# One unit's normed x turned by DMA instead of TensorE, its matmuls one slot later, hash signs behind an eviction

## The chip, the core and the metric

The kernel runs on one core of one Trainium2 chip. Its metric is device time in microseconds: the median of the runs of one program. All numbers without a unit are microseconds. PE is TensorE (PEld its weight loads), DVE is VectorE, ACT is ScalarE, POOL is GpSimd, SP is SyncE, which here issues DMAs.

## The reference

An attention whose scores are masked by a hash, followed by a feed-forward layer. Cut to what is computed:

```
q_bits = (q @ proj > 0); k_bits = (k @ proj > 0)      # 6 bits per token and head
mask   = bucket(q_bits)[:, None] == bucket(k_bits)[None, :]
attn   = softmax(where(mask, q @ k.T / sqrt(64), -1e9))
x      = (attn @ v) of all 8 heads side by side        # 3072 x 512
xn     = x / sqrt(mean(x * x) + 1e-6) * rms_g
out    = (silu(xn @ w_gate) * (xn @ w_val)) @ w_out    # 512 -> 1536 -> 512
```

q, k and v are 4 batches x 8 heads x 768 tokens x 64; everything is f32 outside, f16 in the matmuls inside.

## The kernel before, in words

The work is cut into eight *units* of 384 tokens (half of a batch's 768), numbered 0 to 7. For each unit there is an attention stage of 8 heads and a feed-forward stage.

*Attention.* q and k are loaded by SP, turned so that the 64 features lie on partitions (on TensorE for the first pairs of heads, by DVE for the others: `turn_dve`), and cast to f16 by POOL into the tiles QK. Under the 64 features stand six rows with the hash's sign bits, so that one matmul gives scores and mask together. `hash_one` makes these rows for a pair of heads: four small f32 matmuls into a PSUM bank `d_ps`, one DVE instruction (`signs`) that keeps the sign of each number as f16 (`bits`), and eight small DMAs on SP that put the six rows in place. `scores` is two matmuls into a PSUM tile `s_ps` (two of these tiles exist), `probs` one softmax exponential on ACT (`psb`), `av` eighteen small matmuls for each head into `o_ps` (one such tile), `attn_out` an addition and a reciprocal on DVE (`otmp`, `rcp`) and a product on POOL (`x`).

*Feed-forward.* `norm` takes the sums of squares, a power on POOL and three DVE multiplies that write `xn` (f16, tokens on partitions, one third of 128 tokens at a time). `turn_x` turns one third with four TensorE transposes into a PSUM bank `x_ps`, and moves it into `xnT` while multiplying by rms_g, which lies along partitions in `gcol`. `gate` and `value` are 4 matmuls each for one of 12 column blocks (`g_ps`, `v_ps`, halves of two matmuls), a tanh on ACT (`t`) and two DVE instructions (`a`, `ht`). `project` is 12 matmuls for each third (`y_ps`), `store` a copy on ACT (`ysb`, three buffers) and a DMA on SP. d_ps, x_ps, g_ps, v_ps, y_ps and the mean's m_ps share three PSUM banks in turn.

*What sets the order.* The program is written out in order; each engine runs its own instructions in that order and waits on semaphores. The main loop runs over 192 *slots*, one for each third of a head (two of the six key blocks). A slot emits the scores of the next slot, the exponential of this one, and then what the table `plan` holds for it. While the attention of unit u+1 runs (24 slots from `t0 = NS * (u + 1)`), unit u - 1 is projected and unit u's gates and values are made: first nine pieces of four matmuls of `project(u - 1)`, three for each third, with the turns of unit u behind the seventh and eighth, then 48 half gates and half values of unit u. `spread` deals these pieces to the slots so that each slot gets about the same planned TensorE time; the means and the hashes (`inserts`) are put between pieces at their due slots. The list `late` holds steps that stand behind everything else of their slot, `attn_out` (`o_step`) among them. `norm(u)` stands in slot t0 + 4. Behind the loop come the last products, and unit 7's norm, turn and feed-forward.

SP's queue is in order too: loads, hash rows and stores, each issued when its turn has come and its semaphores allow.

Of the kernel before, what the change touches and what calls it, by code (L numbers as in the profile page):

```python
# [8 lines left out]
FP32 = mybir.dt.float32  # L9
FP16 = mybir.dt.float16  # L10
U16 = mybir.dt.uint16
AF = mybir.ActivationFunctionType
ALU = mybir.AluOpType
# [6 lines left out]
DMODEL = H * D  # L20
DFF = 1536
NF = DFF // 128
HALF = 384
# [10 lines left out]
def kernel(  # L34
# [12 lines left out]
    nc = tc.nc  # L47
    PSUM = bass.MemoryType.PSUM

    const = ctx.enter_context(tc.tile_pool(name="const", bufs=1))  # L50
# [4 lines left out]
    npool = ctx.enter_context(tc.tile_pool(name="npool", bufs=1))  # L55
# [16 lines left out]
    mhalf = const.tile([128, 3], FP32, name="mhalf")  # L72
    ssp = [const.tile([128, 5, 3], FP32, name=f"ssp{i}") for i in range(2)]
    gcol = const.tile([128, 4], FP32, name="gcol")
    wg = const.tile([128, 4, DFF], FP16, name="wg")
    wv = const.tile([128, 4, DFF], FP16, name="wv")
    wo = const.tile([128, NF, DMODEL], FP16, name="wo")
# [5 lines left out]
    def bank(name, shape=None, dt=FP32):  # L83
        return gps.tile(shape or [128, 512], dt, name=name, tag="g")
# [126 lines left out]
    def hash_half(parts):  # L211

        ps = bank("d_ps", [128, HALF])
        for t, src in parts:
            nc.tensor.matmul(  # L215
                ps[32 * t : 32 * t + 32, :], pj[:, 0:32], src,
                start=True, stop=True, tile_position=(0, 32 * t),
            )
        return ps

    def signs(dst, ps):

        upper = ps.bitcast(U16).rearrange("p (c two) -> p c two", two=2)[:, :, 1]
        nc.vector.tensor_scalar(
            out=dst.bitcast(U16), in0=upper, scalar1=SIGN, scalar2=BIT,
            op0=ALU.bitwise_and, op1=ALU.bitwise_or,
        )
# [15 lines left out]
    def hash_direct(b, hp, heads):  # L243
# [34 lines left out]

        return sign, direct, move, send

    def hash_one(b, hp):

        where = ((0, "k", 0), (1, "q", 0), (2, "k", 1), (3, "q", 1))
        ps = hash_half(
            [(t, (qT if which == "q" else kT)[b, hp][:, half * HALF : (half + 1) * HALF])
             for t, which, half in where]
        )
        bt = spool.tile([128, HALF], FP16, name="bits")
        signs(bt, ps)
        for hh in range(2):  # L290
            for t, which, half in where:
                o = (0 if which == "q" else S) + half * HALF
                p0 = 32 * t + 6 * hh
                nc.sync.dma_start(
                    out=QK[b, 2 * hp + hh, "h"][D:KROWS, o : o + HALF],
                    in_=bt[p0 : p0 + 6, :],
                )
# [28 lines left out]
    x, xn, xnT = {}, {}, {}  # L326
# [82 lines left out]

    rstds = {}  # L410

    def norm_scale(u):

        ss = spool.tile([128, 3], FP32, name="ss")
        nc.vector.tensor_reduce(
            out=ss, in_=ssp[u % 2].rearrange("p h c -> p c h"), op=ALU.add, axis=AX.X
        )
        rstd = spool.tile([128, 3], FP32, name="rstd")
        nc.gpsimd.tensor_tensor(out=rstd, in0=ss, in1=mhalf, op=ALU.pow)  # L419
        rstds[u] = rstd  # L420

    def norm(u):
        if u not in rstds:
            norm_scale(u)
        xn[u] = npool.tile([128, 3, DMODEL], FP16, name="xn")
        for c in range(3 if u else 2):
            norm_third(u, c, nc.vector.tensor_scalar_mul)

    def norm_third(u, c, mul):
        mul(xn[u][:, c, :], x[u][:, c, :], rstds[u][:, c : c + 1])  # L430
# [131 lines left out]
    NS = 24  # L562
# [5 lines left out]
    def at(w, s, f, *a):  # L568
        plan[NS * w + s].append(lambda: f(*a))
# [70 lines left out]
    at(0, 1, load_natural, nc.sync, 0, 3, "q")  # L640
    at(0, 2, load_v, nc.sync, 0, 2)
    at(0, 2, load_v, nc.sync, 0, 3)
    at(0, 6, v_prep, 0, 1)
    at(0, 15, v_prep, 0, 2)
    at(0, 19, v_prep, 0, 3, nc.vector)
# [37 lines left out]
    for i, t in ((0, 39), (1, 41), (2, 57), (3, 61)):  # L683
        at(0, t, zero_rows, i)
    TX = 37
    sqs = {}

    def o_step(u, hp, *eng):
# [9 lines left out]
    late = []  # L698
    for n, (u, h) in enumerate(order):
        t = 3 * n + 4 - ((u, h) == (0, H - 1))  # L700
        for part in range(2):
            at(0, t + part, av, u, h, part)
        if h % 2:
            if (u, h) == (0, H - 1):

                at(0, t + 1, o_step, u, h // 2, nc.vector)
                at(0, t + 1, norm_scale, u)
                at(0, t + 1, nc.vector.tensor_scalar_mul, gcol, gcol, float(DMODEL) ** 0.5)
                at(0, t + 2, hash_only, 1, 1)
                at(0, t + 2, hash_signs, 1, 1)  # L710
                at(0, t + 2, norm, u)
                at(0, TX-1, norm_third, u, 2, nc.scalar.mul)
                at(0, TX + 1, send_pair, 1, 1)
                for c in range(3):
                    at(0, TX, turn_x, u, c, c == 2)
                continue
            if (u, h) == order[-1]:
                at(0, t + 1, o_step, u, h // 2, nc.vector)
                continue

            steps = [(t + 1, o_step), (t + (6 if h < 7 else 3), s_step)]
            for s, step in steps:
                if s < 2 * NS or s % NS in (2, 4):
                    at(0, s, step, u, h // 2)
                else:
                    late.append((s, step, u, h // 2))
# [14 lines left out]

    SCORES, AV, PROJ, FEED, TURN, HASH, MEAN = 330, 290, 216, 324, 220, 1000, 120
    inserts = {spot[3]: (HASH, hash_one, *pair) for pair, spot in spots.items()}
    for b in (1, 2, 3):
        for s, hp in ((5, 0), (18, 2)):
            assert 2 * b * NS + s not in inserts
            inserts[2 * b * NS + s] = (MEAN, v_mean, b, hp, 4)

    def spread(t0, n, pieces):
        fixed = [SCORES + (AV if (t - 1) % 3 < 2 else 0) for t in range(t0, t0 + n)]  # L750
        extra = [(t, *inserts.pop(t)) for t in range(t0, t0 + n) if t in inserts]
        total = sum(fixed) + sum(p[0] for p in pieces) + sum(e[1] for e in extra)
        i, done = 0, 0
        for s in range(n):
            done += fixed[s]
            while i < len(pieces):
                weight, whole, steps = pieces[i]
                full = done + weight // 2 > total * (s + 1) // n
                if extra and whole and t0 + s >= extra[0][0] and (full or extra[0][1] > MEAN):
                    _, weight, *step = extra.pop(0)  # L760
                    at(0, t0 + s, *step)
                    done += weight
                    continue
                if full:
                    break
                done += weight
                for delay, *step in steps:
                    at(0, t0 + s + delay, *step)
                i += 1
        for _, _, *step in extra:  # L770
            at(0, t0 + n - 1, *step)
        assert i == len(pieces)

    for u in range(7):
        gates = [
            (FEED, f is gate and part == 0, [(0, f, u, ft, part)])
            for ft in range(NF) for f in (gate, value) for part in range(2)
        ]
        if u == 0:
            t0 = TX + 1  # L780
            spread(t0, 2 * NS - t0, gates)
            continue
        t0 = NS * (u + 1)
        at(0, t0 + 4, norm, u)
        pieces = []
        for i in range(9):
            c, n = divmod(i, 3)
            steps = [(0, project, u - 1, c, 4 * n, 4 * n + 4)]
            if n == 2:
                steps.append((1, store, u - 1, c))  # L790
            pieces.append((4 * PROJ, True, steps))
            if i in (6, 7):
                pieces += [
                    (TURN, False, [(0, turn_x, u, c)]) for c in ((0,), (1, 2))[i - 6]
                ]
        spread(t0, NS, pieces + gates)
    for t, (_, *step) in inserts.items():
        at(0, t, *step)

    for t, *step in late:  # L800
        at(0, t, *step)
# [1 line left out]
    def behind_norm(t):  # L803

        return t - t % NS + 7 if 1 <= t % NS < 7 else t

    for (b, hp), (load, kturns, qturns, _) in spots.items():
# [3 lines left out]
        for w, turns in (("k", kturns), ("q", qturns)):  # L811
            for i, t in enumerate(turns):
                at(0, t, turn_dve, b, hp, w, i, len(turns))
            t = turns[-1] + 1
            at(0, t if (b, hp) == (1, 2) else behind_norm(t), cast_pool, b, hp, w)
        t = 54 if (b, hp) == (1, 2) else behind_norm(qturns[-1] + 2)
# [19 lines left out]
    for c in range(2):  # L836
        project(6, c, 0, NF)
        store(6, c)
    norm(7)
    project(6, 2, 0, 4)  # L840
    for c, f0, f1 in ((0, 4, 6), (1, 6, 8), (2, 8, NF)):
# [41 lines left out]
```

## Time and profile before

| | us |
|---|---|
| median of 3 runs (331.27 to 331.42) | 331.28 |
| the profiled execution, its own time | 330.52 |
| its span, first to last instruction | 328.7 |
| PE busy | 323.0 |
| DVE, ACT, POOL busy | 239.5, 227.2, 158.4 |
| four transposes of x (x_ps) in a row, issue to end | 0.39 |
| move of a turned third on DVE (xnT), median | 0.69 |

A row of the timeline gives start, length, engine, line, operation and tiles; "xN" is how many like instructions were merged in it. The number in square brackets is the idle time of that engine ahead of the row, with what ended it. Matmuls overlap in a pipeline: the length of a merged row is from the first one's start to the last one's end, and the distance of the starts is the time that each takes of PE. Times in the trace count from the span's start. The profiled execution's own time is 1.8 over its span and 0.76 under the median of the other runs.

### The profile page before, as it was taken

To read this page: it belongs to the slowest core of one execution; us is meant where nothing else is said; L and a number is where in the kernel's file an instruction comes from. 1 tells how busy PE (TensorE), PEld (TensorE's weight loads), DVE (VectorE), ACT (ScalarE), POOL (GpSimd) and SP (SyncE) were. 2 spreads that over 40 slices of the span, in tenths; PEclk is the share of its full clock that TensorE was granted. 3 is DMA by queue.
4 is the path that set the end of the run, shared out by engine and by line. 5 is a ranking of instruction groups with operands and counts; after the bars stand their busy time and mean duration, and the time that the engine had idled before them with its cause. 6 is when DMAs were issued, how large, how long until landed. Compare 5 with 4: busy or idle time off the path is not lost.

```text
span 328.7 us, 7869 instructions
## 1 busy us (share of the span) xinstructions
PE 323.0 (98%) x2999; PEld 196.6 (60%) x2999; DVE 239.5 (73%) x526; ACT 227.2 (69%) x331; POOL 158.4 (48%) x204
## 2 busy tenths in 40 slices
PE   8999999999999999999999999999999999999995
PEld 3676666656565566656566565655566566665554
DVE  5887877859888778967888568876768455685860
ACT  7999886766678677775768667785767767744321
POOL 4999759955974542824674521755462111221000
PEclk9999999999999999999999999999999999999999
DMA  7943999988139554432816136001000010002002
GB/s 236 335 158 99 225 211 191 184 157 142 70 58 165 118 114 87 73 77 82 164 21 133 36 93 117 7 3 68 34 5 3 34 64 2 0 2 96 3 1 97
DMA packets 79614, 30.93 MB, mean 94 GB/s; under 512 B 64908, under 2 KB 76632, under 8 KB 79576
## 3 DMA queue, kind: packets, MB, share of 16 engines
q1 hardware_dynamic: 75672, 25.65, 33.2%
q0 software_dynamic: 3680, 4.72, 8.5%
q8 instruction: 23, 0.38, 0.5%
q14 instruction: 15, 0.12, 0.1%
q10 hardware_dynamic: 224, 0.07, 0.1%
HBM read 28.32 MB, written 6.29 MB: 105 GB/s over the span
## 4 chain that ended last, share of the span: by engine, by line
PE 97%; ACT 1%; issue 0%; DVE 0%
PE s_ps L335 20%; PE g_ps L454 19%; PE v_ps L454 19%; PE y_ps L483 18%; PE o_ps L360 11%; PE d_ps L215 2%; PE t_ps L155 2%; PE d_ps L235 2%; PE x_ps L437 2%; PE z_ps L550 1%; ACT psb L347 1%; PE y_ps L502 1%; PE m_ps L319 1%; DVE kT L157 0%; PE s_ps L155 0%
## 5 line engine op out<-in xcount | busy, mean ns | idle before, releaser
L347 ACT ACTIVATE psb<-s_ps,ebias 128x768 f16<-128x768 f32 x192 | 167.7, 899 | 20.8 <-PE s_ps L335 19.9
L335 PE MATMUL s_ps<-QK 128*128 128x384 f16 (+1 forms) x384 | 93.5, 326 | 1.2 <-ACT psb L347 1.1
L462 ACT ACTIVATE t<-g_ps 128x384 f32<-128x384 f32 x96 | 47.1, 491 | 53.0 <-PE g_ps L454 52.9
L454 PE MATMUL g_ps<-xnT,wg 128*128 128x384 f16 x384 | 82.6, 326 | 0.0
L454 PE MATMUL v_ps<-xnT,wv 128*128 128x384 f16 x384 | 81.8, 326 | 0.0
L471 DVE SCALAR_TENSOR_TENSOR a<-t,g_ps 128x384 f32<-128x384 f32 x96 | 52.9, 551 | 27.6 <-ACT t L462 26.0
L381 POOL TENSOR_TENSOR x<-otmp,rcp 128x384 f32<-128x384 f32 x30 | 25.1, 835 | 95.5 <-DVE rcp L379 95.3
L483 PE MATMUL y_ps<-wo,ht 128*128 128x512 f16 x276 | 68.0, 379 | 0.0
L472 DVE SCALAR_TENSOR_TENSOR ht<-a,v_ps 128x384 f16<-128x384 f32 x96 | 53.2, 554 | 11.2 <-PE v_ps L454 2.9
L360 PEld LDWEIGHTS <-psb 128*128 128x128 f16 x1152 | 51.9, 97 | 15.7 <-issue 1.2
L360 PE MATMUL o_ps<-vl,psb 128*128 128x65 f16 x1152 | 55.8, 193 | 0.0
L335 PEld LDWEIGHTS <-QK 128*128 128x128 f16 (+1 forms) x384 | 34.6, 98 | 34.3 <-issue 9.2
L454 PEld LDWEIGHTS <-wv 128*128 128x128 f16 x384 | 35.3, 97 | 21.2 <-issue 0.2
L454 PEld LDWEIGHTS <-wg 128*128 128x128 f16 x384 | 34.8, 97 | 20.8 <-DVE xnT L443 0.4
L483 PEld LDWEIGHTS <-ht 128*128 128x128 f16 x276 | 24.8, 98 | 22.4
L495 ACT COPY ysb<-y_ps 128x512 f32<-128x512 f32 x23 | 13.5, 585 | 19.6 <-PE y_ps L483 19.6
L374 DVE TENSOR_TENSOR otmp<-o_ps,cvb 128x390 f32<-128x390 f32 x32 | 17.8, 557 | 7.6 <-PE o_ps L360 7.6
L207 POOL CAST QK<-qT 64x768 f16<-64x768 f32 x20 | 16.4, 820 | 13.4 <-DVE qT L194 12.8
L430 DVE TENSOR_SCALAR xn<-x,rstd 128x512 f16<-128x512 f32 x23 | 15.8, 738 | 6.8 <-POOL rstd L419 6.8
L387 POOL TENSOR_TENSOR sq<-x 128x384 f32<-128x384 f32 x24 | 19.8, 826 | 1.9
L443 DVE TENSOR_TENSOR xnT<-x_ps,gcol 128x512 f16<-128x512 f16 x22 | 14.5, 686 | 8.0 <-PE x_ps L437 7.9
L207 POOL CAST QK<-kT 64x768 f16<-64x768 f32 x20 | 16.4, 820 | 6.6 <-DVE kT L194 4.7
(83 smaller groups left out, 284.5 us busy)
## 6 DMA issues: line engine op xcount, KB each, us to landing
vn<-in_v_dram SPq DMA_DIRECT2D x16, 384.0 KB
out_dram<-ysb SPq DMA_DIRECT2D x23, 256.0 KB
qL<-in_q_dram SPq DMA_DIRECT2D x40, 96.0 KB
kL<-in_k_dram SPq DMA_DIRECT2D x40, 96.0 KB
kn<-in_k_dram SPq DMA_DIRECT2D x5, 384.0 KB
qn<-in_q_dram SPq DMA_DIRECT2D x5, 384.0 KB
wg<-in_moe_w_gate_dram POOLq DMA_DIRECT2D x2, 768.0 KB, 9.7
wv<-in_moe_w_val_dram POOLq DMA_DIRECT2D x2, 768.0 KB, 11.8
```

Of the source, the lines that this page charges most:

```text
L207: nc.gpsimd.tensor_copy(QK[b, 2 * hp + hh, "h"][0:64, o : o + S], src[64 * hh : 64 * hh + 64, :])
L335: nc.tensor.matmul(ps[:, j, 0:HALF], QK[b, h, "h"][rows, S + jt * 128 : S + (jt + 1) * 128], QK[b, h, "h"][rows, half * HALF : (half + 1) ...
L347: nc.scalar.activation(psb[u, h][:, 2 * ch : 2 * ch + 2, :], sps.pop((u, i))[:, :, 0:HALF], AF.Exp, bias=ebias, scale=ESCALE,)
L360: nc.tensor.matmul(o[:, c, hh, 0:65], psb[u, h][:, jt, c * 128 : (c + 1) * 128], vls[b % 2][:, h, 2 * (jt % 3) + jt // 3 if b in PARITY el ...
L374: nc.vector.tensor_add(tmp[:, :, :, 0:65], o[:, :, :, 0:65], cvb[b % 2][:, 2 * hp : 2 * hp + 2, 0:65].unsqueeze(1).to_broadcast([128, 3, 2 ...
L381: eng.tensor_mul(xd.rearrange("p c (h d) -> p c h d", h=2), tmp[:, :, :, 0:64], r.to_broadcast([128, 3, 2, 64]),)
L387: eng.tensor_mul(sq, xd, xd)
L454: nc.tensor.matmul(ps, w[:, kt, fs], xnT[u][:, kt, :], start=(kt == 0), stop=(kt == 3))
L462: nc.scalar.activation(t, fbank[u, ft, "g_ps"], AF.Tanh, scale=0.5)
L471: nc.vector.scalar_tensor_tensor(out=a, in0=t, scalar=1.0, in1=g, op0=ALU.add, op1=ALU.mult)
L472: nc.vector.scalar_tensor_tensor(out=ht[u][:, ft, :], in0=a, scalar=0.5, in1=vv, op0=ALU.mult, op1=ALU.mult)
L483: nc.tensor.matmul(y, ht[u][:, ft, c * 128 : (c + 1) * 128], wo[:, ft, :], start=(ft == 0), stop=(ft == NF - 1),)
```

## The change

1. Unit 6's normed x is not turned by TensorE. Its three thirds are multiplied by rms_g already in `norm`, by one DVE instruction that takes the row scale and a tile `grow`, and then turned by three DMAs on SP (`turn_dma`, slots t0 + 5 to t0 + 7, t0 = 168), which write `xnT` directly. The twelve transposes and three DVE moves of unit 6 are gone.
2. `grow` is rms_g on all 128 partitions (256 KB), loaded by a DMA on SP in slot 100 and scaled by sqrt(512) on ACT in slot 112.
3. The pieces of the stage in which unit 6 begins are spread from one slot later (169 to 192 instead of 168 to 191), and those of the stage before over 25 slots (144 to 168) instead of 24, by `LAGS`. The twelve gates and values of each unit stay; the turns of unit 6 are no longer pieces.
4. `hash_one` is split: the four matmuls stay in their place, and the sign instruction with its eight DMAs (`hash_bits`) is put on the list `late`, behind what the list already holds for that slot. In the program's order on DVE six of these ten instructions move: four from ahead of a sum-of-squares reduce to behind it, two from ahead of otmp and its reciprocal to behind them.

```diff
--- before.py
+++ after.py
@@ -72,6 +72,7 @@
     mhalf = const.tile([128, 3], FP32, name="mhalf")
     ssp = [const.tile([128, 5, 3], FP32, name=f"ssp{i}") for i in range(2)]
     gcol = const.tile([128, 4], FP32, name="gcol")
+    grow = const.tile([128, DMODEL], FP32, name="grow")
     wg = const.tile([128, 4, DFF], FP16, name="wg")
     wv = const.tile([128, 4, DFF], FP16, name="wv")
     wo = const.tile([128, NF, DMODEL], FP16, name="wo")
@@ -278,13 +279,19 @@
 
         return sign, direct, move, send
 
+    hashed = {}
+
     def hash_one(b, hp):
 
         where = ((0, "k", 0), (1, "q", 0), (2, "k", 1), (3, "q", 1))
-        ps = hash_half(
+        hashed[b, hp] = where, hash_half(
             [(t, (qT if which == "q" else kT)[b, hp][:, half * HALF : (half + 1) * HALF])
              for t, which, half in where]
         )
+
+    def hash_bits(b, hp):
+
+        where, ps = hashed.pop((b, hp))
         bt = spool.tile([128, HALF], FP16, name="bits")
         signs(bt, ps)
         for hh in range(2):
@@ -409,6 +416,16 @@
 
     rstds = {}
 
+    ONDMA = range(6, 7)
+
+    def turn_dma(u, c):
+        if c == 0:
+            xnT[u] = npool.tile([128, 4, HALF], FP16, name="xnT", bufs=2)
+        nc.sync.dma_start_transpose(
+            out=xnT[u][:, :, c * 128 : (c + 1) * 128], in_=xn[u][:, c, :]
+        )
+
+
     def norm_scale(u):
 
         ss = spool.tile([128, 3], FP32, name="ss")
@@ -424,7 +441,13 @@
             norm_scale(u)
         xn[u] = npool.tile([128, 3, DMODEL], FP16, name="xn")
         for c in range(3 if u else 2):
-            norm_third(u, c, nc.vector.tensor_scalar_mul)
+            if u in ONDMA:
+                nc.vector.scalar_tensor_tensor(
+                    out=xn[u][:, c, :], in0=x[u][:, c, :], scalar=rstds[u][:, c : c + 1],
+                    in1=grow, op0=ALU.mult, op1=ALU.mult,
+                )
+            else:
+                norm_third(u, c, nc.vector.tensor_scalar_mul)
 
     def norm_third(u, c, mul):
         mul(xn[u][:, c, :], x[u][:, c, :], rstds[u][:, c : c + 1])
@@ -640,6 +663,8 @@
     at(0, 1, load_natural, nc.sync, 0, 3, "q")
     at(0, 2, load_v, nc.sync, 0, 2)
     at(0, 2, load_v, nc.sync, 0, 3)
+    at(0, 100, nc.sync.dma_start, grow, moe_rms_g.partition_broadcast(128))
+    at(0, 112, nc.scalar.mul, grow, grow, float(DMODEL) ** 0.5)
     at(0, 6, v_prep, 0, 1)
     at(0, 15, v_prep, 0, 2)
     at(0, 19, v_prep, 0, 3, nc.vector)
@@ -683,6 +708,8 @@
     for i, t in ((0, 39), (1, 41), (2, 57), (3, 61)):
         at(0, t, zero_rows, i)
     TX = 37
+
+    LAGS = (0, 0, 0, 0, 0, 1, 1)
     sqs = {}
 
     def o_step(u, hp, *eng):
@@ -746,6 +773,11 @@
             assert 2 * b * NS + s not in inserts
             inserts[2 * b * NS + s] = (MEAN, v_mean, b, hp, 4)
 
+    def place(t, step):
+        at(0, t, *step)
+        if step[0] is hash_one:
+            late.append((t, hash_bits, *step[1:]))
+
     def spread(t0, n, pieces):
         fixed = [SCORES + (AV if (t - 1) % 3 < 2 else 0) for t in range(t0, t0 + n)]
         extra = [(t, *inserts.pop(t)) for t in range(t0, t0 + n) if t in inserts]
@@ -758,7 +790,7 @@
                 full = done + weight // 2 > total * (s + 1) // n
                 if extra and whole and t0 + s >= extra[0][0] and (full or extra[0][1] > MEAN):
                     _, weight, *step = extra.pop(0)
-                    at(0, t0 + s, *step)
+                    place(t0 + s, step)
                     done += weight
                     continue
                 if full:
@@ -768,7 +800,7 @@
                     at(0, t0 + s + delay, *step)
                 i += 1
         for _, _, *step in extra:
-            at(0, t0 + n - 1, *step)
+            place(t0 + n - 1, step)
         assert i == len(pieces)
 
     for u in range(7):
@@ -782,6 +814,9 @@
             continue
         t0 = NS * (u + 1)
         at(0, t0 + 4, norm, u)
+        if u in ONDMA:
+            for c, s in enumerate((5, 6, 7)):
+                at(0, t0 + s, turn_dma, u, c)
         pieces = []
         for i in range(9):
             c, n = divmod(i, 3)
@@ -789,13 +824,14 @@
             if n == 2:
                 steps.append((1, store, u - 1, c))
             pieces.append((4 * PROJ, True, steps))
-            if i in (6, 7):
+            if i in (6, 7) and u not in ONDMA:
                 pieces += [
                     (TURN, False, [(0, turn_x, u, c)]) for c in ((0,), (1, 2))[i - 6]
                 ]
-        spread(t0, NS, pieces + gates)
+        lag, after = LAGS[u - 1 : u + 1]
+        spread(t0 + lag, NS + after - lag, pieces + gates)
     for t, (_, *step) in inserts.items():
-        at(0, t, *step)
+        place(t, step)
 
     for t, *step in late:
         at(0, t, *step)
```

## The prediction

> **What bounds the kernel now.** I read the page first: engine shares, clock and chain.
>
> ```profile
> span 328.7 us, 7869 instructions
> PE 323.0 (98%) x2999; PEld 196.6 (60%) x2999; DVE 239.5 (73%) x526; ACT 227.2 (69%) x331; POOL 158.4 (48%) x204
> PEclk9999999999999999999999999999999999999999
> PE 97%; ACT 1%; issue 0%; DVE 0%
> ```
>
> PE is busy 98% of the span at the full granted clock, and the chain that ended last is 97% PE. A busy PE need not be at its peak, so I looked at the timeline around the place where unit 6's x is turned now (start, length, engine, line).
>
> ```profile
> 263.34 1.28 DVE L430 TENSOR_SCALAR xn<-x,rstd 128x512 f16<-128x512 f32 x3 [0.97 <-POOL rstd L419]
> 265.66 0.39 PE L437 MATMUL x_ps<-ident,xn 128*128 128x128 f16 x4
> 267.35 0.61 PE L437 MATMUL x_ps<-ident,xn 128*128 128x128 f16 x8
> 267.80 1.03 PE L483 MATMUL y_ps<-wo,ht 128*128 128x512 f16 x4
> 268.66 0.49 PE L335 MATMUL s_ps<-QK 128*128 128x384 f16 x2
> 268.98 0.44 PE L360 MATMUL o_ps<-vl,psb 128*128 128x65 f16 x9
> 269.26 0.81 PE L454 MATMUL g_ps<-xnT,wg 128*128 128x384 f16 x4
> ...
> 270.88 0.49 PE L454 MATMUL g_ps<-xnT,wg 128*128 128x384 f16 x2
> 271.44 0.48 PE L335 MATMUL s_ps<-QK 128*128 128x384 f16 x2
> ```
>
> Each row starts where the one before has issued its last matmul: four y take 268.66-267.80 = 0.86, a scores pair 0.32, nine o 0.28, four g or v 0.65. PE loses nothing but between 270.88 and 271.44. So a PE instruction taken away here shortens the run by its issue time, and a wait put in front of PE lengthens it by all of it. ACT shows what the 0.23 before 271.44 is:
>
> ```profile
> 270.11 0.49 ACT L462 ACTIVATE t<-g_ps 128x384 f32<-128x384 f32 x1 [0.66 <-PE g_ps L454]
> 270.49 1.69 ACT L347 ACTIVATE psb<-s_ps,ebias 128x768 f16<-128x768 f32 x2
> ```
>
> The tanh of the first gate stands ahead of a softmax: it starts at 270.11, the softmax at 270.49 ends 0.90 later, and scores two slots on, which overwrite its PSUM, go at 271.44. So from the end of a gate (269.91) to those scores 1.53 must pass; PE had 0.32+0.65+0.32 = 1.30 of work.
>
> Last the queue that gets the work: SP's rows, and DMA share by window (the last two columns).
>
> ```profile
> L496 SPq DMA_DIRECT2D out_dram<-ysb x23: 332/338/1442, 70.8 to 323.3; - x23
> L294 SPq DMA_DIRECT2D QK<-bits x80: 659/667/1319, 78.1 to 244.5; - x80
> 261.00:262.00 1.00, 1.00 (x7) 0.41 (x6) 0.57 (x5) 0.95 (x2) 0.40 (x1) 1.00 0.00 0
> 262.00:263.00 1.00, 1.00 (x14) 0.64 (x13) 0.33 (x3) 0.06 (x1) 0.56 (x1) 1.00 0.68 262
> 263.00:264.00 1.00, 1.00 (x11) 0.50 (x8) 0.66 (x2) 0.84 (x1) 0.30 (x1) 1.00 0.00 0
> ```
>
> A store of 256 KB issued at 261.17 moves in the second after 262 and is through by 263: under 2.0 from issue to landing, with the queue otherwise empty. SP is held 0.33 to 0.67 an issue, at worst 1.3 to 1.4.
>
> **The change part by part.**
>
> *Twelve PE transposes go.* One lasts 219 ns in the rows, but they overlap: eight in 0.61 is (0.61-0.22)/7 = 0.056 each. 12 x 0.056 = 0.67 off PE. The three DVE moves xnT (0.69 each) go too; DVE is not what PE waits for here, so nothing.
>
> *Unit 6's pieces a slot later, unit 5's spread over 25 slots.* The same matmuls in another order; it matters only by where scores meet the softmax. By the rule above I walked the new order. The wait before 271.44 goes (-0.23). The second gate of unit 6 now ends a slot and is followed by scores, nine o and four v, 0.32+0.28+0.65 = 1.25 against 1.53: a new wait of 0.28. A third place, the first scores of a head pair at 245.03, stands 0.12 behind its natural start now (four g and v rows before it end at 244.91); there the new order has 0.3 to spare, -0.12. Net -0.07; between -0.35 (no new wait) and +0.3 (two more).
>
> *The DMAs.* In the new order SP runs the store of unit 5's first third, then three transposes of 128x512 f16 (128 KB each), each behind one third of xn, then the other stores. Queued behind them are only stores, whose ysb has three buffers: nothing. Who waits is the first gate of unit 6, and behind it all of PE, for all three thirds at once. I count from the end of the o's that end unit 6's attention (259.50 now). xn starts 3.84 after it (263.34). Each third now is a multiply of two f32 tensors; the nearest DVE row of 512 elements, xnT with 691 ns, gives 0.69, the next third 0.60 on: ready at 4.53, 5.13, 5.73. PE's order from those o's to the first gate is now 32 y, 7 scores pairs, 4 x 9 o: 32 x 0.2155 + 7 x 0.325 + 4 x 0.28 = 10.3. With h between issues and L from the last issue to landing, the data are there at 4.6+2h+L if h is over 0.6, and in time while 2h+L is under 5.7. No row shows a transposing DMA. Lower bound: h 0.67, L 2.0, sum 3.3, hidden with 2.4 to spare. Upper bound, every 128x128 block paid like a DMA of its own: bits sends follow each other every 0.74 (eight in 5.86), 12 blocks take 8.9, and with 2.0 behind the last the data come at 4.6+11x0.74+2.0 = 14.7, 4.4 late. I take hidden: the row nearest in form and size is the store, twice as many bytes from SBUF by SP, and even with an issue of 1.32, the slowest bits row, and 3.0 to land the sum is 5.6.
>
> Two statements of the Trainium skill pull apart here. VectorE: DVE Perf Modes, The three transpose paths, gives the crossbar DMA 1309 ns for a 128x128 block against 390 on TensorE; my estimate from it, 12 blocks in series, is 15.7, which would end 10 late. DMA: Bandwidth & Descriptors, Latency and other measured facts, gives transposing DMAs an effective 261 GB/s, an estimated 1.5 for the three. No run here shows either yet.
>
> *grow.* A 256 KB broadcast by SP at slot 100 delays loads that have tens of microseconds; its scaling on ACT at slot 112 (128x512, 0.73 by the xn row of ACT) falls behind the softmax at 167.43, where ACT idles 0.62 before the tanh at 168.94 and the next instruction may start 0.48 after such a copy (264.08, 264.56). Cost 0; at most the 0.11 that it is over the gap.
>
> *Signs.* Six of the ten sign instructions move: four behind a reduce (0.53), two behind otmp and its reciprocal (0.75). Their d_ps bank is wanted three banks on, some 3 later, and the sends have about ten slots. The list of waits shows no PE wait for either now, so 0 gain and, with DVE's queue at 73%, a bound of 0.2 loss.
>
> Sum: -0.67-0.07 = -0.74, rounded to -0.73 for grow's bound. The profiled execution took 330.52, 0.76 under the median of 331.28: 329.79 there, 330.55 against the median. What a measurement can tell from no change is 0.2%, 0.66: the forecast lies just past it.
>
> **The rivals.**
>
> *The first gate waits for the transposes* (slower). Place: g_ps at the head of unit 6. It decides from 2h+L = 5.7; the run is slower than before once the data are over 0.73 late, and by over 0.2% past 1.4. For it: four blocks to a DMA, a form that the kernel never issued, and all three needed at once. Against: six times the fixed cost is left. With blocks paid singly, 4.4 late: 331.28-0.73+4.4 = 334.9. With h of 2.2, 2h+L = 6.4, 0.7 late: 331.3. Chance 0.24, two thirds of it past the 0.2%.
>
> *Every block in series, at the longest issue that SP shows* (1319 ns, a bits row): 12 x 1.32 = 15.8, the data at 4.6+15.8 = 20.4, 10.1 late, 331.28-0.73+10.1 = 340.7. For it: nothing in the rows but that one length; against: the median issue of the same rows is half of it, a store's a quarter, and a store's 128 rows of 2 KB go out together. Chance 0.03. The Trainium skill's 1309 ns for a block (the section above) is this rule.
>
> *PE's saving is given back* (within 0.2%): ACT is 69% busy and several scores in units 5 and 6 start under 0.15 behind their softmax, so two or three new waits of 0.2 to 0.3 take most of the 0.67. Against: a slot of PE is 1.5 and ACT's share of it 1.2, so one wait hides the next. 331.1. Chance 0.10.
>
> **How the numbers follow.** Forecast 0.63, rivals 0.24, 0.03, 0.10. Inside the forecast, -0.73 with some 0.25 either way, two thirds lie past -0.66: faster 0.42, same 0.21. The late rival gives same 0.08 and slower 0.16; the series 0.03 slower; the giving back 0.06 same and 0.04 slower. Faster 0.42, same 0.35, slower 0.23. The range runs from the forecast with no new ACT wait (330.2) to a first gate 1.65 late (332.2); past it lies most of the late rival, 0.17.
>
> **What would show it.** After, no x_ps row stands between unit 5's last y and unit 6's first g. Right: that g follows its scores pair at once, and SP's three transposes lie over 1 ahead of it. Wrong: PE idle ahead of that g, put down to a DMA of xnT. Also: a scores wait of about 0.28 two slots on, none at 245; no wait at grow's slot; bits rows later with PE gapless. The prediction fails if SP is held about 2 by each transpose, or if the order wakes more softmax waits than the one found.

## The result, and the profile after

The changed kernel took 329.81 us (median of 6 runs, 329.42 to 330.41) against 331.24 for the kernel before beside it (6 runs, 330.92 to 331.42): 1.43 less by the medians. The ratio is 0.9965, 95% interval 0.9954 to 0.9975, so 0.8 to 1.5 us faster. The forecast was 330.55, with a range from 330.2: the sign was right, the size about half of what came.

The page of the changed kernel (the profiled execution took 330.41, 0.60 over its median, so spans are not compared directly below):

```profile
span 328.6 us, 7853 instructions
PE 323.6 (98%) x2986; PEld 196.2 (60%) x2987; DVE 238.5 (73%) x523; ACT 227.8 (69%) x332; POOL 158.4 (48%) x204
PE 98%; ACT 1%; issue 0%
```

PE has 13 matmul records fewer, 12 of them the transposes, and still is the chain. Its busy time is not smaller: the first microseconds ran at half pace for longer in this execution (last section). So the gain has to be read stretch by stretch. The timeline of PE where unit 6's turns used to be (start, length, engine, line):

```profile
268.92 1.03 PE L506 MATMUL y_ps<-wo,ht 128*128 128x512 f16 x4
269.78 0.49 PE L342 MATMUL s_ps<-QK 128*128 128x384 f16 x2
270.10 0.81 PE L477 MATMUL g_ps<-xnT,wg 128*128 128x384 f16 x4
270.75 0.49 PE L477 MATMUL v_ps<-xnT,wv 128*128 128x384 f16 x2
271.08 0.49 PE L342 MATMUL s_ps<-QK 128*128 128x384 f16 x2
...
272.65 0.49 PE L342 MATMUL s_ps<-QK 128*128 128x384 f16 x2
272.98 0.44 PE L367 MATMUL o_ps<-vl,psb 128*128 128x65 f16 x9
273.25 0.81 PE L477 MATMUL v_ps<-xnT,wv 128*128 128x384 f16 x4
274.19 0.48 PE L342 MATMUL s_ps<-QK 128*128 128x384 f16 x2
```

No x_ps row is left, and the first gate at 270.10 follows its scores pair after 0.32, without idle time: the transposes were there. The lost time is now between 273.25 and 274.19: four v take 0.65, so 0.28 is a wait. ACT's rows say for what:

```profile
272.85 0.49 ACT L485 ACTIVATE t<-g_ps 128x384 f32<-128x384 f32 x1 [0.62 <-PE g_ps L477]
273.24 1.69 ACT L354 ACTIVATE psb<-s_ps,ebias 128x768 f16<-128x768 f32 x2
```

A tanh ahead of a softmax, as before the change, but two slots on: this is the new wait that the forecast named. The queue that got the work, SP, and DVE's new norm:

```profile
262.69 0.34 SPq L519 DMA_DIRECT2D out_dram<-ysb  x1
264.48 3.94 SPq L424 DMA_TRANSPOSE xnT<-xn  x3
268.51 2.41 SPq L519 DMA_DIRECT2D out_dram<-ysb  x2
```

```profile
263.67 2.08 DVE L445 SCALAR_TENSOR_TENSOR xn<-x,rstd,grow 128x512 f16<-128x512 f32 x3 [0.97 <-POOL rstd L436]
```

```profile
L424 SPq DMA_TRANSPOSE xnT<-xn x3: 1205/1211/1327, 264.5 to 267.2; - x3
```

The last line is the group view of the tile xnT (shortest, median and longest in ns). Each transpose holds SP for 1.2 to 1.3. They were issued at 264.48, 265.91 and 267.21, and their semaphores rose at 267.06, 268.36 and 269.65: 2.44 behind the last issue, 0.45 ahead of the gate that reads them.

**Where the time went.** The time until slot 24 differs from execution to execution (29.34 in the profile before, 30.42 in the one after), so I compare distances inside one execution. From the start of the scores of slot 144 (216.18 before, 217.37 after) to the first gate of unit 7 (301.45, 302.02) PE needs 85.27 before and 84.65 after: 0.62 less. From slot 24 to slot 144 the kernels agree within 0.11. From PE's last start (325.06 and 325.62) to the end of the span (328.74 and 328.63) it takes 3.68 before and 3.01 after: another 0.67. The forecast had no term for that second place.

### The profile page after: what moved, and what is told of

It reads as the page before. It is cut to its first block, busy times and chain, and to the rows that moved or that the text cites. A ratio compares the mean times of both kernels' runs of the same rounds, so it can differ in the third digit from the quotient of the medians.

```text
span 328.6 us, 7853 instructions
## 1 busy us (share of the span) xinstructions
PE 323.6 (98%) x2986; PEld 196.2 (60%) x2987; DVE 238.5 (73%) x523; ACT 227.8 (69%) x332; POOL 158.4 (48%) x204
## 4 chain that ended last, share of the span: by engine, by line
PE 98%; ACT 1%; issue 0%
PE s_ps L342 20%; PE g_ps L477 19%; PE v_ps L477 19%; PE y_ps L506 18%; PE o_ps L367 11%; PE d_ps L216 2%; PE t_ps L156 2%; PE d_ps L236 2%; PE x_ps L460 1%; PE z_ps L573 1%; ACT psb L354 1%; PE y_ps L525 1%; PE m_ps L326 1%; PE s_ps L156 0%; ACT t L485 0%
## 5 line engine op out<-in xcount | busy, mean ns | idle before, releaser
L453 DVE TENSOR_SCALAR xn<-x,rstd 128x512 f16<-128x512 f32 x20 | 14.5, 777 | 5.9 <-POOL rstd L436 5.9
L466 DVE TENSOR_TENSOR xnT<-x_ps,gcol 128x512 f16<-128x512 f16 x19 | 12.6, 687 | 7.0 <-PE x_ps L460 6.8
```

## Experiments

Eleven runs were made, in three groups. Each was timed against the kernel before on the same chip; the ratio goes by those pairs, and differences of medians against those in its group (331.23, 331.27 and 331.0) can differ from it by some 0.2 us.

**1. The two kernels again.** The kernels themselves, unedited, to see how much an execution's own start moves the result.

> The kernel before, unchanged, against itself. Theory A (the change's own worth is the 0.62 that PE's rows lose between the scores of slot 144 and unit 7's first gate; the rest of the measured 1.43 lies in how the first 24 us and the last stores of an execution fall out): ratio 1.000 within 0.2%, and a profile whose PE marks from slot 60 on keep the distances of the profile before within 0.1, while the start (clock opening) and the end (last store to end) move by up to 1. Theory B (the runs of before were drawn from slower executions): ratio off 1 by 0.2% or more.

> The changed kernel again. Theory A: -0.5 to -0.8 us on the median once start and end are averaged (ratio 0.998). Theory C (something in the change is worth 1.4 in every execution, such as an earlier start or an earlier end): ratio 0.9955 to 0.9965 again.

Measured: 331.17 for the kernel before (ratio 1.0002, 0.9991 to 1.0012) and 329.76 for the one after (0.9951, 0.9938 to 0.9964). So the change is worth 1.4 again, and it isn't the luck of one execution: for the second run theory A, with 0.5 to 0.8, was wrong, and theory C is the one that fits. The same marks: slot 144 to unit 7's first gate 85.30 and 84.65; PE's last start to the end 3.80 and 3.01. Both places show again. From slot 24 to slot 144 the two profiles of the kernel after differ by 0.29 (186.95 and 187.23), so that stretch is less steady than these two.

**2. The moved signs, taken out and alone.** In the first the sign instruction stands right behind its matmuls again and all else is as after; in the second only the signs are moved.

```diff
 # e3: the kernel after
         if step[0] is hash_one:
-            late.append((t, hash_bits, *step[1:]))
+            at(0, t, hash_bits, *step[1:])
 # e4: the kernel after, without DMA turns, lag and grow
-    ONDMA = range(6, 7)
+    ONDMA = range(0)
-    LAGS = (0, 0, 0, 0, 0, 1, 1)
+    LAGS = (0, 0, 0, 0, 0, 0, 0)
```

> The changed kernel with the signs back in their old place, behind their matmuls, and all else kept. My theory: the moved signs are worth 0, so this is as fast as the changed kernel within 0.1 us. Rival: the signs behind otmp give back the part of the gain that PE's rows do not show (0.5 to 0.8), so this is 0.5 to 0.8 slower than the changed kernel.

> The kernel before with the signs moved and nothing else. My theory: 0 within 0.1 us, PE's order being the same instruction for instruction. Rival: 0.5 to 0.8 faster.

Measured: 329.88 (0.9961, 0.9947 to 0.9974) without the move, 331.16 (1.0004, 0.9991 to 1.0017) with the move alone. In the traces the stretch of units 5 and 6 is 0.62 shorter in the first and unchanged in the second, the end 3.03 and 3.88. The moved signs are worth nothing, as forecast.

**3. The end of the kernel.** Here is what ends before and after, in the view of SP's waits (line, cause: sum, times, longest):

```profile
SPq L878 <- DMA out_dram<-ypart: 1.8, 3, 1.0
```

```profile
SPq L914 <- DMA out_dram<-ypart: 1.4, 3, 0.6
```

The first line is of the kernel before, the second of the one after; 878 and 914 are the lines with which the kernels end. The last store, in the timeline before and after:

```profile
325.61 0.35 ACTq L508 DMA_DIRECT2D out_dram<-ypart  x1
```

```profile
326.17 0.34 ACTq L531 DMA_DIRECT2D out_dram<-ypart  x1
```

SP's last work is to wait for the eight semaphores on which the transfers of SP and ACT complete, always in the order 0 to 7, one instruction for each, about 0.06 apart. The transfers take those semaphores in turn. In the kernel before SP and ACT issue 236 transfers together, and the last store (ACT's, of ypart) lies on semaphore 3: four waits follow its own. In the kernel after they issue 240, and the store lies on 7: none follows. Besides, the store lands later in the kernel before: 1.99 from its issue until SP goes on, against 1.56; while it is under way the trace has a packet of 8192 bytes that fetches instructions (326.38 to 326.87).

Two kernels shift this rotation by four and do nothing else: four loads of one number each.

```diff
+    tiny = const.tile([1, 4], FP32, name="tiny")
...
+    for i in range(4):
+        at(0, 102 + i, nc.sync.dma_start, tiny[:, i : i + 1], moe_rms_g[i : i + 1].partition_broadcast(1))
```

> The kernel before, with added work: four loads of one number each from the sync queue at slots 102 to 105, into a tile that nothing reads. They move no work of any engine; they shift by four the rotation in which the sync and scalar queues' transfers take the eight completion semaphores, so that the kernel's last store completes on semaphore 7, as in the kernel after, and no longer on 3. Theory E (half of the gain lies at the end: sync's waits for the eight semaphores go in order, and whatever semaphore the last store lies on decides how many follow it): from the start of the last matmul to the end of the span 3.0 to 3.4 us in place of 3.7 to 3.9, so 0.25 to 0.8 off the time, 330.4 to 331.0 us. Theory W (the whole 1.43 lies in units 5 and 6, the end's shorter tail being what an execution happened to have): no change, 331.1 to 331.3.

> The kernel after with the same four added loads, which put its last store back on semaphore 3. Theory E: the tail grows from 3.0 to 3.3 to 3.9 us, and 0.3 to 0.8 of the 1.43 is given back: 330.1 to 330.6 us. Theory W: no change, 329.7 to 329.9.

Measured: with four loads more the kernel before takes 330.43 (11 runs, 0.9975, 0.9965 to 0.9985), 0.84 less by the medians. The kernel after takes 330.14 with them (6 runs, 0.9968, 0.9957 to 0.998) in place of 329.8 in the other groups, so 0.3 of its gain is gone. From slot 24 to PE's last start the first is within 0.01 of the kernel before: nothing but the end has changed. Theory E holds: four small loads whose data nothing reads made the kernel before faster. For the kernel after, the 0.3 alone would not be clear of the noise, since its two ratios' intervals overlap (0.9954 to 0.9975 without the loads); its trace has the end longer by 0.25 (3.27 against 3.01).

The two shares were told apart with eight such loads, which bring the rotation back to semaphore 3 and only make SP's program longer.

```diff
+    tiny = const.tile([1, 8], FP32, name="tiny")
...
+    for i in range(8):
+        at(0, 102 + i, nc.sync.dma_start, tiny[:, i : i + 1], moe_rms_g[i : i + 1].partition_broadcast(1))
```

> The kernel before with eight added loads of one number each from the sync queue, at slots 102 to 109: the rotation of the completion semaphores comes round to where it was, so the last store lies on semaphore 3 and four waits follow it, as in the kernel before; only sync's program is longer. It tells apart the two shares of the longer tail, the four waits (0.25) and the later landing of the last store (1.97 to 2.26 us from its issue in place of 1.55 to 1.58), beside whose packets the trace shows an instruction-fetch packet of 8192 bytes. Theory F (the packet belongs to sync's program, and its time goes by the program's length: 326.4 in the kernel before, 325.6 with four loads more): the packet comes before the last store's, the landing takes 1.6, the tail is 3.25 to 3.3 us, and the time 330.6 to 330.9. Theory K (the late landing is tied to the kernel before or to semaphore 3): tail 3.7 to 3.9, time 331.1 to 331.4.

Measured: 330.55 against 331.0 (0.9988, 0.9979 to 0.9997), with an end of 3.27: theory F fits. The ends side by side, from the traces:

| kernel | semaphore of the last store | issue until SP goes on | last 8192-byte fetch | PE's last start to the end |
|---|---|---|---|---|
| before | 3 | 1.99 | 326.38 to 326.87, beside the store | 3.68 |
| before, again | 3 | 2.11 | 326.92 to 327.51, beside the store | 3.80 |
| before + 8 loads | 3 | 1.57 | 319.78 to 320.09 | 3.27 |
| after + 4 loads | 3 | 1.58 | 319.30 to 319.79 | 3.27 |
| before + 4 loads | 7 | 1.58 | 325.60 to 325.93, ahead of the store | 3.03 |
| after | 7 | 1.56 | 319.92 to 320.23 | 3.01 |

Semaphore 3 instead of 7 costs 0.24 to 0.25: four waits of 0.06. The late landing costs 0.4 to 0.5 more (3.68 and 3.80 against 3.27), and it went when nothing but SP's program had grown; the packet went with it. Late landing and packet come together in all four traces that have a packet beside the last store, those of the two experiments with the longest ends (moved signs alone 3.88, turns on TensorE 3.94) among them. The traces also show what is late: a transfer's completion comes as sixteen updates of its semaphore, and in these four fifteen come within 0.17 and a single one 0.30 to 0.57 behind them (before: 327.11 to 327.28, then 327.58). In the kernel before with four loads, whose packet runs earlier, a store ahead of the last has such a straggler (326.66, then 326.84) and the last has none; no last store of the other traces has one. So the packet goes with one held-up sixteenth of a transfer; that both were on the same DMA engine the traces do not tell, and no run moved the packet alone.

**4. The lag.** The kernel after with unit 6's gates where they were; the transposes stay.

```diff
-    LAGS = (0, 0, 0, 0, 0, 1, 1)
+    LAGS = (0, 0, 0, 0, 0, 0, 0)
```

> The kernel after with unit 6's gates not a slot later (all lags zero), the transposes on the sync queue where they are. Theory D (the lag is what hides the transposes): the first gate of unit 6 would stand at about 268.3 to 268.6 on TensorE while the last of the three transposes lands at 269.65, so TensorE idles 1.0 to 1.4 us ahead of it; against that the two new waits of 0.28 each in units 5 and 6 may go. 330.2 to 331.2 us. Theory N (the gate does not need the transposes so early, or other waits in the unit take the idle time back): 329.2 to 329.8.

Measured: 331.58 (11 runs; 1.0009, 0.9998 to 1.0019), 1.8 more than the kernel after and slightly above the range of either theory. PE's timeline:

```profile
268.19 0.49 PE L342 MATMUL s_ps<-QK 128*128 128x384 f16 x2
268.52 0.44 PE L367 MATMUL o_ps<-vl,psb 128*128 128x65 f16 x9
270.29 0.81 PE L477 MATMUL g_ps<-xnT,wg 128*128 128x384 f16 x4 [1.33 <-DMA xnT<-xn]
```

The square bracket is the late rival of the forecast: PE is idle for 1.33 ahead of the first gate, and the profile puts it down to the DMA of xnT; the gate starts 1.49 later than it would right behind the o's. Theory D holds, its size was short: by the trace the stretch from slot 144 to unit 7's first gate is 86.14, 1.49 more than in the kernel after. I had set the two waits of 0.28 against the idle time. They do go, but those at 245 (0.12) and at the hash (0.17) are back, and one of 0.28 stands ahead of the scores at 287.76. The slot of lag is what hides the transposes.

**5. The turns back on TensorE, with lag and moved signs.**

```diff
-    grow = const.tile([128, DMODEL], FP32, name="grow")
+    grow = None
...
-    ONDMA = range(6, 7)
+    ONDMA = range(0)
...
-    at(0, 100, nc.sync.dma_start, grow, moe_rms_g.partition_broadcast(128))
-    at(0, 112, nc.scalar.mul, grow, grow, float(DMODEL) ** 0.5)
```

> The kernel after without the transposing DMAs and without the load of g's row: unit 6's twelve transposes are TensorE's again, the lag and the moved signs stay. Theory E and the prices read from the traces: twelve pitches of 0.056 come back (0.67) between units 5 and 7, the waits that the lag made or took away stay (the sum of the rest there is +0.05), and the last store lies on semaphore 3 again (0.3 to 0.8): 330.7 to 331.3 us, so nearly the time before. Theory W (the lag and the order are worth more than the turns): 330.2 to 330.5, with an unchanged tail of 3.0.

Measured: 331.65 (11 runs; 1.0012, 1.0001 to 1.0023), above the range given. The stretch of units 5 and 6 is 85.53, 0.88 more than in the kernel after. Of that 0.67 are the transposes; the other 0.21 is the lag's order, which with the turns in it waits in yet other places: the wait of 0.28 near 243 stays, the other of 0.28 is gone, one of 0.23 stands ahead of the scores at 285.11, and three gates and values start 0.13, 0.08 and 0.06 late (the first, at 270.81, behind the last move of xnT on DVE, which ends at 270.76). And the end is 3.94. So the lag without the DMAs makes units 5 and 6 longer than before by 0.26; theory E's prices held for the turns, not for the rest of the order, which I had taken over unchanged.

**6. More units.** The same treatment for units 5 and 6, and for 4 to 6, with five and two one-number loads so that the last store lies on 7.

```diff
 # e10
-    ONDMA = range(6, 7)
+    ONDMA = range(5, 7)
-    LAGS = (0, 0, 0, 0, 0, 1, 1)
+    LAGS = (0, 0, 0, 0, 1, 1, 1)
 # e11: range(4, 7) and (0, 0, 0, 1, 1, 1, 1)
```

> The kernel after with unit 5's normed x turned by DMAs as well, its gates also a slot later, and five added loads of one number each, so that the last store lies on semaphore 7 as in the kernel after. Theory G (what unit 6 gave in its own stretch, 0.62, repeats: twelve pitches of 0.056 less a wait or two of 0.28): 329.0 to 329.5 us. Theory Q (in unit 5 the sync queue and the DMA engines have hash rows besides, the transposes land after their gate, and TensorE waits for them as in the run with no lag): 330.2 or more.

> The same for units 4, 5 and 6, with two added loads of one number each, which put the last store on semaphore 7. Theory G: a further 0.4 to 0.67, 328.4 to 329.1 us. Theory Q: the transposes of unit 4 come late as well, 330.5 or more.

Measured: 332.25 (5 runs; 1.0038, 1.0025 to 1.005) and 334.92 (4 runs; 1.0121, 1.0107 to 1.0134). Theory Q holds for both. PE's waits in the second (cause: sum, times, longest), then SP's rows in its unit 4:

```profile
PE g_ps L478 <- DMA xnT<-xn: 2.3, 2, 1.7
...
PE d_ps L217 <- DVE qT L196: 0.5, 1, 0.5
PE d_ps L217 <- DVE a L495: 0.4, 1, 0.4
```

```profile
188.76 2.63 SPq L425 DMA_TRANSPOSE xnT<-xn  x2
191.49 0.52 SPq L520 DMA_DIRECT2D out_dram<-ysb  x1
192.11 1.23 SPq L425 DMA_TRANSPOSE xnT<-xn  x1
```

The first gate waits 1.7 in unit 4 and 0.57 in unit 5. In unit 4 it starts at 196.19, 4.08 behind the issue of the third transpose; in unit 6 of the kernel after the third took 2.44 to land. Fifteen of this transpose's sixteen updates come by 194.44, just before the gate would have started (194.49), and one at 196.15; a packet of 16384 bytes that fetches instructions runs from 193.87 to 195.09. This is the picture of the kernel's end again, a straggler beside a fetch, here in one trace. In unit 5 the hash rows on SP stand in the way, in the run with units 5 and 6:

```profile
224.46 3.62 SPq L302 DMA_DIRECT2D QK<-bits  x5
228.18 0.39 SPq L520 DMA_DIRECT2D out_dram<-ysb  x1
228.67 3.95 SPq L425 DMA_TRANSPOSE xnT<-xn  x3
```

SP sends hash rows and a store until 228.57, so the first transpose is issued 2.47 behind the start of xn (226.20) in place of 0.81; the third lands 2.32 behind its issue, no slower than in unit 6, and PE idles 0.64 ahead of the gate. The three xn took DVE longer there too (3.56 in place of 2.08), but each was done 1.18 or more before its transpose went out, so it was the queue that set the issues. Beyond the turns, the shifted order lets matmuls of the hash wait for DVE (0.5 and 0.4) and once those of a value (0.7), which they don't in the kernel after; why DVE is slower in these units was not separated. No version that ran is faster than the kernel after.

## Why the prediction was right and wrong

*Twelve transposes, -0.67: right.* Slot 144 to unit 7's first gate fell by 0.61 to 0.62 against the profile before in all four traces of kernels in which unit 6 alone is turned by DMA, with the lag; the missing transposes, twelve times the 0.056 between two starts, take 0.67 off, and the order gives some back. The run with the turns on TensorE has them back.

*The order, -0.07: right in all three places that it named, wrong in that there were five.* The wait before 271.44 is gone (-0.23), the one at 245.03 is gone (-0.12), the new one two slots behind the second gate measured 0.28, as forecast. Two were not seen. Ahead of 243.99 nine o's now wait for otmp, which reads their only PSUM tile and stands on DVE behind an ht:

```profile
243.39 0.49 PE L342 MATMUL s_ps<-QK 128*128 128x384 f16 x2
243.99 0.43 PE L367 MATMUL o_ps<-vl,psb 128*128 128x65 f16 x9
```

```profile
242.82 0.56 DVE L495 SCALAR_TENSOR_TENSOR ht<-a,v_ps 128x384 f16<-128x384 f32 x1
243.29 0.56 DVE L381 TENSOR_TENSOR otmp<-o_ps,cvb 128x390 f32<-128x390 f32 x1
```

The scores pair has issued after 0.32, at 243.71, and the o's go at 243.99, behind otmp's end at 243.85: +0.28. And the hash matmuls at 237.60, which waited for DVE's qT, come half a slot later and find it ready: -0.17. The five are +0.04 together (+0.05 by the stretch), so this term missed by some 0.12. That it missed by no more is partly luck: the two that were not seen have opposite signs. The walk of the order had followed the softmax alone; DVE's order belonged into it.

*The DMAs hidden: right, by 0.45.* The condition was that 2h+L stay under 5.7. Measured: h 1.37 between issues, L 2.44, so 5.17, with 0.45 left at the gate. The estimate's upper value for a store-like row (1.32, and 3.0 to land: 5.6) was near. The "six times the fixed cost" that was held against the late rival stands in no row: by the lower bound's own sum of 3.3, the 5.7 was 1.7 times what was needed. Of the two statements of the Trainium skill that the forecast set against each other neither gives the time here. The Trainium skill, VectorE: DVE Perf Modes, The three transpose paths, has 1309 ns for a 128x128 block; here four blocks together hold SP for 1205 to 1327 ns. The Trainium skill, DMA: Bandwidth & Descriptors, Latency and other measured facts, has 261 GB/s, by which the estimate was 1.5 for the three; they took 5.17 from the first issue to the last landing. The late rival is real: without the lag PE idles 1.33 for it, in unit 4 1.7.

*grow and signs, 0: right.* From slot 96 to slot 120 the kernels agree to 0.01, though grow's scaling stands in between; the signs are experiment 2.

*The step that failed.* "Queued behind them are only stores, whose ysb has three buffers: nothing." The prediction put what the added DMAs do to SP's queue at nothing, and its sum -0.67-0.07 took the end of the kernel as given. For the stores' start that is true. But four DMAs more on SP (three transposes and grow) also moved which semaphore the last store completes on, and the last store no longer has an instruction fetch beside it. Measured, that is -0.67 in the two profiles and -0.79 in their repetitions, of which 0.25 are the four waits and the rest the earlier landing. With -0.62 and -0.65 in units 5 and 6 it makes -1.29 and -1.45, against 1.43 between the medians. The term was missing because no step of the forecast looked at what SP does behind its last transfer. So half of the gain has nothing to do with turning x: the kernel before gets 0.84 from four loads that nothing reads.

## What to carry to other kernels

Where an added transfer looks free, follow it to the kernel's end too: the waits there go through the completion semaphores in a fixed order, so the number of transfers decides how many follow the last store, and it can be padded with tiny loads. A transfer that replaces work on the bounding engine must be timed against its reader in every stage where it is used; what had 0.45 to spare in unit 6 was 0.6 and 1.7 late in units 5 and 4, once because other transfers stood ahead of it in its queue. When an order shifts by a slot, follow every engine that frees a single-buffered tile, not only the one that limited the old order.

## What was not expected of the hardware

- A transposing DMA of 128x512 f16 (four 128x128 blocks) holds the issuing queue 1.2 to 1.33 and lands 2.44 after the last of three issues; its traffic is 1536 packets of 256 bytes for the three, 18 ns each.
- The start of an execution moves by itself. In the thirteen traces PE reaches slot 24 up to 1.09 later than in the earliest, with no relation to the edit (before 29.34, before again 29.84, after 30.42, after again 29.42). It mostly goes with how long TensorE stays at half pace at the start: until 3.65 in the kernel before by its clock record, until between 6.06 and 6.80 in the profile after by the lengths of its hash matmuls (0.82 to 0.85, later 0.51). It isn't all of it: the kernel before with four loads is at full pace from 3.71 and reaches slot 24 at 29.91. The Trainium skill, TensorE: Matmul & The Clock Gate, Part 1: The HAM clock gate, says that the warm-up varies between runs of one kernel; the traces agree, with clock records that open at 3.65 and at 4.48 for the kernel before. A difference of 0.5 between two profiled spans is therefore no reading; distances between two marks inside one execution can agree to 0.01 (slot 96 to 120: 39.25 to 39.26 in twelve of the thirteen), though not in every stretch (slot 24 to 60: 52.98 to 53.39).
- Waits on completion semaphores at the end cost 0.06 each even where they are long satisfied. And a fetch of instructions beside a transfer goes with one of its sixteen completion updates being late, by 0.30 to 0.57 at the kernel's end and by 1.7 in unit 4 of the run with units 4 to 6.
